# A new order list for the same operations in a fused retention and SwiGLU kernel

## The chip, the cores and the metric

The kernel runs on one core of a Trainium2 chip. A core has five engines with a queue each: TensorE (PE; its weight loads are listed apart as PEld), VectorE (DVE), ScalarE (ACT), GpSimd (POOL) and SyncE (SP), which here only issues transfers. The metric is the device time of one execution in microseconds (us); lower is better. The engines run their own lists in order and wait for each other through semaphores.

## The reference

```python
# q, k, v: (4 batches, 8 heads, 768 steps, 64), float32
state = gamma[None, :, None, None] * state + np.einsum('bhd,bhe->bhde', k[:, :, t], v[:, :, t])
y[:, :, t] = scale * np.einsum('bhd,bhde->bhe', q[:, :, t], state)
...
# x: y as (3072 tokens, 512)
rms = np.sqrt(np.mean(x * x, axis=-1, keepdims=True) + 1e-06)
xn = x / rms * rms_g
g = xn @ w_gate                       # 512 -> 1536
silu = g * (1.0 / (1.0 + np.exp(-g)))
return (silu * (xn @ w_val) @ w_out)  # 1536 -> 512
```

A recurrence with a decay gamma for each head, then a root-mean-square norm and a gated feed-forward layer.

## The kernel before, in words

The 768 steps are cut into six chunks c of 128 steps. Within a chunk the recurrence is computed in parallel form: scores of q against k under a decaying causal mask, times v, plus q times the state that earlier chunks left. A chunk has four batches b of 128 rows, so a tile is 128 rows by 512 columns (eight heads of 64). The feed-forward layer takes a chunk's four batches together: 512 rows. Its hidden width of 1536 is cut into 12 blocks n of 128.

There is no loop over this work. A string, ORDER (lines 17 to 99), is a list of 865 words, each one operation; a loop at the end (L604) takes word by word and emits its instructions. A word such as `v.0.0.2.2.3/4` has the operation, its indices and after a slash the PSUM banks; `@D`, `@A`, `@P` and `@S` name the engine (DVE, ACT, POOL, SP). The list thus sets, for every engine, the order of its queue. The words, with the lines that emit them:

- `Lq`, `Lk`, `Lv` c.b (L301 to L314): load q, k or v. On SP as float32 (tiles qf, kf, vf), on POOL with a cast to bf16 on the way (qb, kb, vp). For chunk 0, q and k that come through POOL are loaded in an eight-row form (L312) that needs a sort on PE.
- `Ck`, `Cq`, `V` (L335, L344, L350): casts of what SP loaded, with the decay for q and v from chunk 2 on.
- `Tk`, `Tq` (L362): transposes or sorts on PE, `Ek`, `Eq` (L375) copy the result out of PSUM as kT, qT. `tk`, `tq` (L386) are transposes by DMA, issued on SP. `J` (L507) turns a sorted kT back.
- `A` (L397) scores on PE, `M0` and `M1` (L422) the masked scores on DVE, `Y` (L433) and `Z` (L409) the outputs y on PE.
- `S`, `R`, `N` (L450, L462, L474): sum of squares on ACT, reciprocal root on POOL, normed row xn on DVE. `X` (L492) transposes xn on PE and `XE` (L499) copies it out; from chunk 2 on `XE@S` is a DMA transpose instead.
- `D` (L514) decayed k on DVE or POOL, `K` (L522) the new state's part on PE, `U` (L533) its sum and `B` (L541) its bf16 copy.
- `wg`, `wv`, `wo` (L323, L331): loads of the weights on POOL, in pieces. Every load of chunk 2 waits for the last piece of `wo` (L318).
- `g`, `v` c.n0.n1.b0.b1 (L548): feed-forward matmuls with the gate and value weights; `s` (L560) the silu on ACT, `h` (L566) the product on DVE. A stretch of blocks and batches can be cut small, so that it can start when one batch and one piece of weights are there.
- `d` (L574) the down projection on PE, `o` (L582) its copy out of PSUM, `st` (L589) the store by SP. `e` (L597) is the down projection of the last output block, cut into three column pieces.
- `H.n` (L236): n filler matmuls of 512 columns on PE that compute nothing that is used. `G` (L293) and `GE` spread the norm's weight over the rows. `causal`, `iota`, `ident`, `vd`, `yd`, `yt`, `mk0`, `mk1`, `mc`, `tab` make masks, decays and load the activation table.

Of the kernel before, what the change touches and what calls it, by code (L numbers as in the profile page):

```python
# [27 lines left out]
v.0.0.4.3.4/1 s.0.0.4.3.4 h.0.3.4.0.3 g.0.4.6.3.4/0 v.0.2.3.0.3/4 h.0.0.4.3.4 h.0.2.3.0.3 wg.9.12 g.0.5.6.0.3/5
s.0.4.6.3.4 D.0.2@P Lk.1.0@P B.0.0 g.0.4.5.0.3/7 s.0.5.6.0.3 wv.9.12 Tk.1.2/1 h.0.5.6.0.3 s.0.4.5.0.3
g.0.8.9.0.4/3 v.0.4.6.3.4/4 K.0.2.2/7 Tq.1.1/2 wo.0.4 g.0.6.7.0.4/0 Lv.1.1@P h.0.4.6.3.4 Ek.1.2@A g.0.7.8.0.4/1  # L30
Eq.1.1@D mc.1@D U.0.2.2@D h.0.4.5.0.3 D.1.1@P B.0.3 s.0.8.9.0.4 Tq.1.0/5 v.0.6.7.0.4/2 Tq.1.2/7 v.0.8.9.0.4/6
s.0.7.8.0.4 Eq.1.0@D Eq.1.2@D s.0.6.7.0.4 h.0.6.7.0.4 v.0.7.8.0.4/4 h.0.8.9.0.4 Lv.1.2@P A.1.2/70
g.0.10.11.0.4/6 Tk.1.0/1 Ek.1.0@A B.0.2 h.0.7.8.0.4 g.0.9.10.0.4/4 Lv.1.0@P M0.1.2 s.0.10.11.0.4 s.0.9.10.0.4
A.1.0/3572 M1.1.0 g.0.11.12.0.4/6 wo.4.8 M1.1.2 v.0.11.12.0.4/5 v.0.10.11.0.4/0 B.0.1 M1.1.1 wo.8.12
s.0.11.12.0.4 v.0.9.10.0.4/2 Lk.1.3@P Lq.1.3@P Lv.1.3@P d.0.1.0.4/4 h.0.11.12.0.4 Lq.2.0@S M0.1.1 Y.1.1/1
K.1.1/5 M0.1.0 S.1.1 h.0.10.11.0.4 Y.1.2/7 S.1.2 R.1.1 R.1.2 Lk.2.1@S D.1.0@P d.0.0.0.4/0 U.1.1@D Lk.2.3@S
h.0.9.10.0.4 Y.1.0/5 d.0.3.0.4/6 S.1.0 N.1.1 N.1.2 R.1.0 X.1.1/2 XE.1.1@D Lq.2.3@S d.0.2.0.4/3 D.1.2@P X.1.2/7
XE.1.2@A N.1.0 d.0.2.4.8 d.0.0.4.8 d.0.1.4.8 X.1.0/5 B.1.1 XE.1.0@D d.0.1.8.12 Lk.2.0@S o.0.1@A d.0.0.8.12
Tk.1.3/4 Ek.1.3@D g.1.0.1.0.3/1 v.1.0.1.0.3/2 Lq.2.1@S Tq.1.3/7 Eq.1.3@D o.0.0@A d.0.2.8.12 Lv.2.1@S K.1.0/4
s.1.0.1.0.3 h.1.0.1.0.3 A.1.3/51 M0.1.3 Ck.2.1@A tk.2.1 d.0.3.4.8 M1.1.3 g.1.3.4.0.3/7 Cq.2.0@P Y.1.3/0  # L40
s.1.3.4.0.3 U.1.0@D S.1.3 d.0.3.8.12 R.1.3 v.1.2.3.0.3/4 g.1.2.3.0.3/2 N.1.3 Lq.2.2@S o.0.3@A s.1.2.3.0.3
g.1.1.2.0.3/7 Ck.2.0@P X.1.3/5 s.1.1.2.0.3 h.1.2.3.0.3 Cq.2.3@D v.1.3.4.0.3/2 v.1.1.2.0.3/4 Lk.2.2@S XE.1.3@A
g.1.9.10.0.4/0 h.1.1.2.0.3 o.0.2@D h.1.3.4.0.3 g.1.5.6.0.4/5 Cq.2.1@P v.1.9.10.0.4/7 g.1.7.8.0.4/4 tq.2.0
Lk.3.0@S D.1.3@D g.1.11.12.0.4/3 v.1.7.8.0.4/6 V.2.1@D B.1.0 tq.2.1 s.1.5.6.0.4 tk.2.0 s.1.9.10.0.4 Ck.2.2@P
v.1.5.6.0.4/1 Ck.2.3@A Lq.3.0@S h.1.5.6.0.4 s.1.7.8.0.4 s.1.11.12.0.4 Lq.3.1@S Cq.2.2@P v.1.11.12.0.4/2 tk.2.3
tq.2.3 h.1.7.8.0.4 Ck.3.0@P h.1.9.10.0.4 g.1.6.7.0.4/0 h.1.11.12.0.4 s.1.6.7.0.4 v.1.6.7.0.4/3 Lv.2.0@S K.2.1/1
h.1.6.7.0.4 K.1.2.2/7 tq.2.2 A.2.0/2564 U.1.2.2@D g.1.0.4.3.4/3 M1.2.0 M1.2.1 Cq.3.1@P M0.2.1 v.1.8.9.0.4/0
g.1.8.9.0.4/5 g.1.4.5.0.4/6 Lk.3.1@S s.1.0.4.3.4 B.1.2 B.1.3 s.1.8.9.0.4 M0.2.0 tk.2.2 Y.2.1/3 S.2.1 h.1.8.9.0.4
v.1.0.4.3.4/4 v.1.4.5.0.4/0 U.2.1@D s.1.4.5.0.4 Cq.3.0@P R.2.1 v.1.10.11.0.4/6 g.1.10.11.0.4/2 h.1.4.5.0.4
h.1.0.4.3.4 Ck.3.1@P V.2.0@A N.2.1 tk.3.0 Y.2.0/5 s.1.10.11.0.4 h.1.10.11.0.4 Lv.2.2@S tq.3.1 A.2.2/4301  # L50
Lv.2.3@S M0.2.2 tk.3.1 V.2.2@P S.2.0 Lq.3.2@S M1.2.2 M0.2.3 d.1.1.0.10/2 d.1.1.10.12 M1.2.3 Y.2.2/3 R.2.0 S.2.2
d.1.2.0.12/1 N.2.0 R.2.2 V.2.3@D Y.2.3/4 d.1.0.0.10/0 XE.2.1@S Cq.3.2@P d.1.0.10.12 o.1.2@A S.2.3 N.2.2 R.2.3
# [587 lines left out]
```

## Time and profile before

| | |
|---|---|
| median of 3 runs (lowest to highest) | 232.96 us (232.46 to 233.1) |
| the profiled execution | 233.88 us |
| its span, first to last instruction | 232.1 us |
| TensorE busy | 224.2 us |
| granted TensorE clock, mean | 1.000 |
| moved between HBM and chip | 28.31 MB read, 6.29 MB written |

The profile is one execution. A row of the time line has the start, the duration, the engine and line, the operation with what it writes and reads, and how many; in brackets the idle time before it and what ended that. Durations of matmuls overlap, since PE is a pipeline: their pace is read from start to start. The chain of waits is followed back from the last instruction and has start, duration, engine, tile and line.

### The profile page before, as it was taken

What the parts mean: (1) busy time and instruction counts of PE and PEld (TensorE: products, weight loads), DVE (VectorE), ACT (ScalarE), POOL (GpSimd) and SP (SyncE); (2) the same over time, 40 slices, a digit from 0 to 9 for tenths busy, and PEclk for the clock granted to TensorE, in tenths of its full rate; (3) what the DMA queues carried; (4) which work ended last, traced back from release to release, by engine and by line L of the source; (5) the groups of instructions that cost most, each with busy time, mean ns of one, the idle gap of its engine ahead of it and who ended that gap; (6) DMA issues with size and microseconds to landing.
All of it is one profiled execution on the core that took longest, in us unless ns stands there. A gap on an engine that the chain in (4) does not pass through costs nothing.

```text
span 232.1 us, 4715 instructions
## 1 busy us (share of the span) xinstructions
PE 224.2 (97%) x1819; PEld 118.1 (51%) x1843; DVE 128.0 (55%) x233; ACT 90.1 (39%) x211; POOL 95.7 (41%) x169
## 2 busy tenths in 40 slices
...
DMA  6999999999879796989969769993861410001232
GB/s 121 150 168 157 187 182 187 199 179 227 182 158 139 158 219 105 240 172 227 197 138 222 205 129 198 248 133 70 123 197 23 120 64 0 0 0 48 109 133 76
DMA packets 105352, 33.60 MB, mean 145 GB/s; under 512 B 94449, under 2 KB 102385, under 8 KB 105330
## 3 DMA queue, kind: packets, MB, share of 16 engines
...
HBM read 28.31 MB, written 6.29 MB: 149 GB/s over the span
## 4 chain that ended last, share of the span: by engine, by line
PE 89%; POOL 3%; DVE 3%; DMA 3%; issue 1%; ACT 0%; POOLq 0%
PE g_ps L553 26%; PE o_ps L578 26%; PE v_ps L553 26%; DMA kb<-in_k_dram 3%; PE y_ps L442 2%; PE a_ps L405 2%; PE y_ps L446 2%; PE kv_ps L529 1%; PE o_ps L600 1%; POOL qb L312 1%; PE xt_ps L496 1%; DVE qT L382 1%; POOL vp L314 1%; DVE hT L571 1%; PE t_ps L373 1%
## 5 line engine op out<-in xcount | busy, mean ns | idle before, releaser
L571 DVE TENSOR_TENSOR hT<-sg,v_ps 128x512 bf16<-128x512 bf16 (+2 forms) x76 | 48.5, 655 | 52.9 <-PE v_ps L553 28.3
L563 ACT ACTIVATE sg<-g_ps 128x512 bf16<-128x512 f32 (+2 forms) x76 | 42.1, 574 | 77.9 <-PE g_ps L553 67.3
L553 PE MATMUL g_ps<-xnT,wg_b 128*128 128x512 bf16 (+2 forms) x335 | 70.0, 343 | 0.7 <-DVE hT L571 0.2
L553 PE MATMUL v_ps<-xnT,wv_b 128*128 128x512 bf16 (+2 forms) x336 | 69.9, 344 | 0.4
L578 PE MATMUL o_ps<-wo_b,hT 128*128 128x512 bf16 x269 | 63.0, 379 | 0.4
L553 PEld LDWEIGHTS <-wv_b 128*128 128x128 bf16 x344 | 30.7, 98 | 29.4 <-issue 0.2
L553 PEld LDWEIGHTS <-wg_b 128*128 128x128 bf16 x344 | 30.6, 98 | 29.5 <-DVE st_f L538 0.2
L578 PEld LDWEIGHTS <-hT 128*128 128x128 bf16 x276 | 26.2, 98 | 29.6 <-PE o_ps L578 0.5
L483 DVE SCALAR_TENSOR_TENSOR xn<-y_ps,rstd,g_bc 128x512 bf16<-128x512 f32 x22 | 16.5, 748 | 18.0 <-POOL rstd L471 18.0
L469 POOL TENSOR_SCALAR ms<-ssq 128x1 f32<-128x1 f32 x24 | 4.5, 190 | 46.3 <-ACT xsq L459 45.6
L427 DVE TENSOR_TENSOR am<-a_ps,causal 128x512 bf16<-128x512 f32 x32 | 20.2, 682 | 5.3 <-PE a_ps L405 5.3
L145 ACT COPY o_sb<-o_ps 128x512 f32<-128x512 f32 (+2 forms) x16 | 8.6, 549 | 37.2 <-PE o_ps L578 32.8
L545 POOL CAST st_b<-st_f 64x256 bf16<-64x256 f32 x40 | 17.3, 431 | 8.8 <-DVE st_f L538 6.3
L341 POOL TENSOR_TENSOR qb<-qf,ydec 128x512 bf16<-128x512 f32 x14 | 14.9, 1063 | 12.9 <-DMA qf<-in_q_dram 12.7
L459 ACT ACTIVATE xsq<-y_ps 128x512 f32<-128x512 f32 x22 | 13.1, 596 | 13.1 <-PE y_ps L446 12.7
L471 POOL TENSOR_TENSOR rstd<-ms,mhalf 128x1 f32<-128x1 f32 x24 | 13.2, 551 | 2.0
L145 DVE COPY o_sb<-o_ps 128x512 f32<-128x512 f32 (+1 forms) x10 | 6.5, 653 | 11.0 <-PE o_ps L578 8.2
L427 DVE TENSOR_TENSOR am<-a_ps,mask 128x512 bf16<-128x512 f32 x16 | 10.3, 683 | 2.7 <-PE a_ps L405 2.7
L145 POOL CAST kb<-kf 128x512 bf16<-128x512 f32 x9 | 5.9, 660 | 10.1 <-DMA kf<-in_k_dram 10.0
L442 PEld LDWEIGHTS <-am 128*128 128x128 bf16 x176 | 7.7, 98 | 3.9 <-issue 0.3
L442 PE MATMUL y_ps<-vp,am 128*128 128x64 bf16 x176 | 8.9, 193 | 0.2
L360 POOL TENSOR_TENSOR vp<-vf,vdec 128x512 bf16<-128x512 f32 x7 | 7.7, 1105 | 2.9 <-DMA vf<-in_v_dram 2.8
...
## 6 DMA issues: line engine op xcount, KB each, us to landing
out_dram<-o_sb SPq DMA_DIRECT2D x23, 256.0 KB, 2.5
kf<-in_k_dram SPq DMA_DIRECT2D x17, 256.0 KB, 3.8
vf<-in_v_dram SPq DMA_DIRECT2D x17, 256.0 KB, 4.0
qf<-in_q_dram SPq DMA_DIRECT2D x16, 256.0 KB, 3.4
...
qb<-in_q_dram POOLq DMA_DIRECT2D x8, 128.0 KB, 6.1
kb<-in_k_dram POOLq DMA_DIRECT2D x7, 128.0 KB, 6.2
vp<-in_v_dram POOLq DMA_DIRECT2D x7, 128.0 KB, 6.3
```

The costliest lines, as they stand in the source:

```text
L145: (e.copy if e is ACT else e.tensor_copy)(out, in_)
L341: e.tensor_tensor(out=u["qb"], in0=u["qf"], in1=ydec[:, c, :, None].to_broadcast([128, H, D]), op=ALU.mult)
L427: DVE.tensor_tensor(out=u["am"][:, i], in0=u["a"][i], in1=m, op=ALU.mult)
L442: nc.tensor.matmul(y[:, h, :], u["am"][:, h % 2, h // 2, :], u["vp"][:, h, :], start=h == 0, stop=c == 0 and h == H - 1, skip_group_check= ...
L459: ACT.activation(xsq, flat(u["y"]), AF.Square, accum_out=u["ssq"])
L471: POOL.tensor_tensor(out=u["rstd"], in0=ms, in1=mhalf, op=ALU.pow)
L483: DVE.scalar_tensor_tensor(out=u["xn"], in0=flat(u["y"]), scalar=u["rstd"], in1=g_bc, op0=ALU.mult, op1=ALU.mult)
L545: POOL.tensor_copy(st_b[b][r, :, i * 64:i * 64 + 64], st_f[b // 2][r, b % 2])
L553: nc.tensor.matmul(p[:, (n - n0) * m:(n - n0 + 1) * m], W[w][0][:, s, n * 128:(n + 1) * 128], xnT[c][:, s, b0 * C:b1 * C], start=s == 0, s ...
L563: ACT.activation(sg[:, :cols], done["wg", c, n0, b0][:, :cols], AF.Silu)
L571: DVE.tensor_tensor(out=hT[c][:, n0:n1, b0 * C:b1 * C], in0=sg, in1=p, op=ALU.mult)
L578: nc.tensor.matmul(o_ps[c, b], hT[c][:, n, b * C:(b + 1) * C], wo_b[:, n, :], start=n == 0, stop=n == NFF - 1)
```

## The change

Only ORDER changes: 867 words instead of 865. The operations on data are the same; order, banks and, for some fifty of them, the engine are others. The words that are not in both: fillers (`H`) are 17 matmuls before and 23 after.

The head of the list, cut to its start (the words up to the first feed-forward matmul and the first of those behind it):

```diff
-Lk.0.2@S causal Lv.0.2@S>causal rms.1@S Ck.0.2@D H.8/1 ident Lq.0.2@P vd Lk.0.1@P Lq.0.1@P Tk.0.2/2 Lq.0.0@P
-H.1/0 H.4/0 Tq.0.2/7 G/1 yd iota yt Lk.0.0@P mk0 Tk.0.1/6 Ek.0.2@D Lv.0.1@P mk1 Eq.0.2@D A.0.2/32 Lv.0.0@P
-Lk.0.3@P Tq.0.0/4 Tq.0.1/7 Lq.0.3@P GE@A M0.0.2 V.0.2@A wv.0.2 M1.0.2 wg.0.2 Ek.0.1@A Tk.0.0/1 Eq.0.1@A Eq.0.0@A
-Lk.1.1@P J.0.1/6 Y.0.2/5 Ek.0.0@D D.0.1@D S.0.2 R.0.2 A.0.0/0731 Lv.0.3@P M0.0.0 M1.0.0 H.2/2 Tk.0.3/2 tab
-M1.0.1 H.1/7 Y.0.0/7 Ek.0.3@A M0.0.1 H.1/2 Tq.0.3/2 N.0.2 J.0.0/3 S.0.0 Eq.0.3@A Y.0.1/0 wg.2.4 X.0.2/4 A.0.3/52
-R.0.0 N.0.0 J.0.3/1 XE.0.2@D S.0.1 X.0.0/6 wv.4.6 M1.0.3 v.0.0.2.2.3/4 R.0.1 g.0.0.2.2.3/7 XE.0.0@A Tk.1.1/6
...
+Lk.0.2@S H.4/4 yd causal Lv.0.2@S>causal yt rms.1@S ident Ck.0.2@A Lq.0.0@P H.8/1 Lq.0.1@P Lq.0.2@P Tk.0.2/7
+H.2/5 Lk.0.0@P Tq.0.1/0 vd Tq.0.0/4 Ek.0.2@D Lk.0.1@P Tq.0.2/1 Lk.0.3@P G/7 V.0.2@D Eq.0.1@D Tk.0.0/0 Tk.0.1/6
+Eq.0.2@D Eq.0.0@D iota Lq.0.3@P A.0.2/31 Lv.0.1@P mk0 Lv.0.0@P Lv.0.3@P Ek.0.0@D mk1 GE@A wg.0.2 M1.0.2 wv.0.2
+H.2/4 M0.0.2 Ek.0.1@A A.0.0/5270 D.0.2@P M1.0.1 Tk.0.3/6 Y.0.2/1 Tq.0.3/0 M0.0.1 H.2/4 tab Lk.1.1@P M1.0.0
+M0.0.0 S.0.2 Ek.0.3@A J.0.0/4 J.0.1/7 R.0.2 Y.0.1/2 Eq.0.3@A S.0.1 H.1/6 H.3/0 H.1/5 D.0.0@D Y.0.0/3 N.0.2
+J.0.3/5 D.0.1@D wv.2.4 R.0.1 X.0.2/6 N.0.1 S.0.0 wg.2.4 A.0.3/41 R.0.0 X.0.1/0 XE.0.2@A wg.4.6 D.0.3@D M0.0.3
+XE.0.1@A g.0.0.2.2.3/2 K.0.2.2/5 K.0.0.2/6 M1.0.3 U.0.2.2@A s.0.0.2.2.3 N.0.0 v.0.0.2.2.3/7 g.0.0.2.1.2/0
...
```

As the queues see it: POOL issues q of batches 0, 1 and 2, then k of 0, 1 and 3, q of 3, the three v, and then wg and wv (before: q 2, k 1, q 1, q 0, k 0, v 1, v 0, k 3, q 3, wv, wg, and v of 3 after k of the next chunk). The first twelve operations of PE are fillers. Later in the list:

- POOL's order of the remaining loads after k of chunk 1's batch 1: `wv.2.4 wg.2.4 wg.4.6 Lq.1.0 wv.4.6 wg.6.9 wv.6.9 Lk.1.2 Lk.1.0 wg.9.12 Lq.1.1 Lq.1.2 wv.9.12 wo.0.4 Lv.1.1 Lv.1.0 wo.4.8 wo.8.12 Lv.1.2 Lq.1.3 Lk.1.3 Lv.1.3`; before: `Lv.0.3 wg.2.4 wv.4.6 wv.2.4 wg.4.6 Lk.1.2 wg.6.9 Lq.1.1 wv.6.9 Lq.1.0 Lq.1.2 wg.9.12 Lk.1.0 wv.9.12 wo.0.4 Lv.1.1 Lv.1.2 Lv.1.0 wo.4.8 wo.8.12 Lk.1.3 Lq.1.3 Lv.1.3`.
- `mc.1` goes from DVE to POOL, `U.0.0.2` and `U.0.2.2` from DVE to ACT; `D.1.0` from POOL to DVE; `Ek.1.0` and `Ek.1.2` from ACT to DVE.
- On SP, chunk 4's four `XE@S` stand later among chunk 5's transposes: `XE.4.0 tq.5.1 tq.5.0 tk.5.1 XE.4.3 XE.4.2 XE.4.1 tk.5.0` (before: `XE.4.0 XE.4.1 XE.4.2 XE.4.3 tq.5.1 tk.5.0`, a v load, `tq.5.0 tk.5.1`). In the list two PE words (`v.4.8.9.0.4`, `Y.5.2`) stand between `tk.5.0` and `A.5.0`; before, `Y.5.2` and two feed-forward words stood between `tk.5.1` and `A.5.0`.
- The tail ends `d.5.2.0.12`, `e.5.3.0` (before: `d.5.2.0.12`, `e.5.3.2`, `e.5.3.0`).

More of the change, by code (lines that the diff above doesn't have):

```diff
@@ L28 @@
[L28 to L52, printed above, removed]
@@ new lines @@
+s.0.0.2.0.1 X.0.3/6 v.0.0.2.0.1/5 XE.0.3@A Lk.1.0@P B.0.0 wg.9.12 s.0.3.4.0.3 Lq.1.1@P g.0.5.6.0.3/1
+g.0.2.3.0.3/7 h.0.3.4.0.3 s.0.2.3.0.3 Lq.1.2@P h.0.2.3.0.3 g.0.4.5.0.3/0 wv.9.12 h.0.0.2.0.1 s.0.4.5.0.3
+v.0.0.4.3.4/2 g.0.0.4.3.4/7 v.0.4.5.0.3/3 mc.1@P s.0.5.6.0.3 s.0.0.4.3.4 h.0.0.4.3.4 wo.0.4 v.0.5.6.0.3/4
+h.0.5.6.0.3 D.1.1@P Lv.1.1@P h.0.4.5.0.3 Lv.1.0@P g.0.8.9.0.4/7 g.0.6.7.0.4/0 mc.0@D s.0.8.9.0.4 v.0.4.6.3.4/4
+g.0.4.6.3.4/5 s.0.4.6.3.4 v.0.8.9.0.4/6 D.1.0@D D.1.2@P wo.4.8 s.0.6.7.0.4 Tk.1.2/2 Ek.1.2@D Tq.1.0/5
@@ new lines @@
+N.1.1 d.0.1.0.4/0 R.1.0 d.0.2.0.4/5 N.1.0 X.1.1/3 d.0.2.4.8 d.0.0.4.8 Lv.1.3@P d.0.3.4.8 X.1.0/7 d.0.3.8.12
+XE.1.0@A Y.1.2/2 Tq.1.3/7 d.0.0.8.12 S.1.2 d.0.1.4.8 Lq.2.0@S XE.1.1@D o.0.0@A Eq.1.3@D o.0.3@A R.1.2 N.1.2
+Tk.1.3/1 d.0.2.8.12 X.1.2/3 Ek.1.3@A Ck.2.2@P D.1.3@D Lq.2.1@S A.1.3/17 XE.1.2@A M1.1.3 K.1.0/4 K.1.2.2/6
+K.1.1/2 B.0.3 M0.1.3 Lq.2.2@S tk.2.2 Ck.2.0@A g.1.0.1.0.3/3 v.1.2.3.0.3/7 U.1.1@D Y.1.3/1 s.1.0.1.0.3
+g.1.1.2.0.3/3 S.1.3 Lk.2.1@S g.1.3.4.0.3/2 o.0.2@A R.1.3 U.1.2.2@D d.0.1.8.12 Cq.2.1@P s.1.3.4.0.3 U.1.0@D
@@ new lines @@
+g.1.10.11.0.4/5 Cq.3.1@D Lv.2.2@S v.1.11.12.0.4/7 Cq.2.3@P h.1.5.6.0.4 s.1.11.12.0.4 B.1.3 h.1.11.12.0.4
+v.1.10.11.0.4/0 s.1.10.11.0.4 s.1.4.5.0.4 h.1.10.11.0.4 v.1.4.5.0.4/4 Cq.3.0@P h.1.4.5.0.4 g.1.7.8.0.4/5
+Lk.3.0@S A.2.0/4726 tq.2.3 tq.2.2 M0.2.0 v.1.7.8.0.4/0 Lv.2.3@S tq.3.1 Lk.3.2@S M0.2.1 s.1.7.8.0.4 M1.2.1
+g.1.6.7.0.4/1 h.1.7.8.0.4 M1.2.0 V.2.1@P v.1.6.7.0.4/5 Y.2.1/4 Ck.3.0@A s.1.6.7.0.4 S.2.1 K.2.1/0 tk.3.1 K.2.0/6
+V.2.2@P h.1.6.7.0.4 A.2.2/7231 M0.2.3 d.1.1.0.10/5 Lk.3.3@S V.2.3@P M1.2.3 tq.3.0 M1.2.2 d.1.1.10.12 R.2.1
@@ new lines @@
+M1.3.3 v.2.9.10.0.4/6 tk.4.1 g.2.10.11.0.4/7 Y.3.1/0 Cq.4.2@P h.2.0.1.0.4 s.2.9.10.0.4 S.3.1 Y.3.2/2
+s.2.10.11.0.4 st.1.0@S h.2.9.10.0.4 S.3.2 V.4.0@P h.2.4.5.0.4 Lq.4.3@S v.2.10.11.0.4/3 Lq.4.1@S Y.3.3/5 R.3.1
+h.2.10.11.0.4 v.2.11.12.0.4/1 N.3.1 S.3.3 g.2.11.12.0.4/4 s.2.11.12.0.4 R.3.2 Lv.5.1@S d.2.1.0.10/6 K.3.2.2/3
+R.3.3 N.3.2 XE.3.0@S K.3.0.2/0 Lk.4.0@S XE.3.2@S N.3.3 XE.3.1@S Lv.4.3@S XE.3.3@S h.2.11.12.0.4 Ck.4.0@A
+d.2.3.0.12/1 d.2.2.0.12/2 U.3.0.2@D g.3.0.1.0.4/4 v.3.0.1.0.4/7 Lq.4.0@S U.3.2.2@D st.0.2@S g.3.3.4.0.4/0
@@ new lines @@
+Ck.4.2@P s.3.3.4.0.4 st.0.1@S Lk.4.3@S Lv.5.0@S g.3.5.6.0.4/3 st.1.1@S B.3.1 v.3.3.4.0.4/0 d.2.1.10.12 tk.4.2
+g.3.4.5.0.4/5 Cq.4.3@P Cq.4.1@D s.3.0.1.0.4 Lq.5.3@S o.2.3@A h.3.0.1.0.4 h.3.3.4.0.4 s.3.5.6.0.4 o.2.1@D
+g.3.1.2.0.4/3 v.3.1.2.0.4/1 s.3.1.2.0.4 Ck.5.0@D o.2.2@D B.3.2 tq.4.2 V.4.3@P g.3.6.7.0.4/4 Lq.5.2@S V.4.2@P
+Cq.4.0@P v.3.6.7.0.4/3 s.3.6.7.0.4 tq.4.0 h.3.1.2.0.4 v.3.5.6.0.4/0 g.3.2.3.0.4/2 h.3.5.6.0.4 Lk.5.1@S
+h.3.6.7.0.4 tk.4.0 s.3.4.5.0.4 V.5.2@P tq.4.1 s.3.2.3.0.4 v.3.2.3.0.4/4 g.3.9.10.0.4/1 Ck.4.3@D v.3.4.5.0.4/0
@@ new lines @@
+g.4.5.6.0.4/2 v.4.9.10.0.4/4 v.4.1.2.0.4/7 XE.5.0@S st.3.3@S v.4.4.5.0.4/6 h.4.9.10.0.4 g.4.4.5.0.4/0
+s.4.1.2.0.4 g.5.3.4.0.4/3 st.3.0@S g.5.11.12.0.4/5 s.4.5.6.0.4 v.4.5.6.0.4/1 h.4.1.2.0.4 s.5.3.4.0.4
+g.5.9.10.0.4/3 g.5.0.1.0.4/2 s.4.4.5.0.4 h.4.5.6.0.4 g.5.7.8.0.4/1 s.5.7.8.0.4 v.5.7.8.0.4/0 h.5.7.8.0.4
+v.5.3.4.0.4/1 g.4.6.7.0.4/4 v.5.11.12.0.4/7 h.4.4.5.0.4 st.2.2@S h.5.3.4.0.4 s.5.11.12.0.4 s.4.6.7.0.4
+v.5.0.1.0.4/1 g.5.6.7.0.4/4 s.5.0.1.0.4 h.5.0.1.0.4 h.5.11.12.0.4 g.5.2.3.0.4/0 v.4.6.7.0.4/7 v.5.9.10.0.4/2
```

94 lines of the change are left out of this document (44 added, 50 removed).

## The prediction

> **What bounds the kernel now.** First the page's busy table, its DMA slices and its chain by engine: they name the bound and show where there is room.
>
> ```profile
> span 232.1 us, 4715 instructions
> PE 224.2 (97%) x1819; PEld 118.1 (51%) x1843; DVE 128.0 (55%) x233; ACT 90.1 (39%) x211; POOL 95.7 (41%) x169
> DMA  6999999999879796989969769993861410001232
> PE 89%; POOL 3%; DVE 3%; DMA 3%; issue 1%; ACT 0%; POOLq 0%
> ```
>
> PE is busy 97% of the span and carries 89% of the chain. The DMA row stands at 9 from slice 2 to slice 11, 6 to 64 us (a slice is 5.8 us): while weights and first inputs arrive, PE and the transfers are both full. Second, PE in order of time at the start.
>
> ```profile
> 1.11 3.59 PE L239 MATMUL hot_ps<-one 128*128 128x512 bf16 x8 [1.11 <-DVE one L152]
> 7.35 0.44 PE L368 MATMUL t_ps<-pick,qb 128*64 128x64 bf16 x16
> 7.72 1.12 PE L295 MATMUL g_row_ps<-g_row,ones 1*128 1x512 f32 x2
> 8.77 0.44 PE L368 MATMUL t_ps<-pick,kb 128*64 128x64 bf16 x16
> 9.15 0.40 PE L405 MATMUL a_ps<-qT,kT 64*128 64x128 bf16 x8
> 13.48 0.44 PE L368 MATMUL t_ps<-pick,kb 128*64 128x64 bf16 x16 [0.73 <-DMA kb<-in_k_dram]
> 17.52 0.61 PE L553 MATMUL v_ps<-xnT,wv_b 128*128 128x128 bf16 x8
> ```
>
> Until 17.52 PE runs fillers (L239) and the short attention work of chunk 0; from there a nearly unbroken line of matmuls to the tail. The order list gives both kernels the same work on PE except for fillers, 17 before and 23 after, all ahead of the first feed-forward matmul; and at that matmul both have done the same attention work (eight sorts of q and k, three J, all four A, three Y, two X). What PE has left there is equal. So the end moves by three amounts: the start of that matmul, what PE loses behind it, and the tail.
>
> Third, the chain of waits and PE's own rows where most is lost behind 17.52.
>
> ```profile
> 31.50 0.69 DVE qT L382
> 32.19 1.29 DVE mask L281
> ...
> 33.50 0.68 DVE st_f L145
> ...
> 37.09 1.02 PE g_ps L553 x4
> ...
> 39.19 0.55 PE a_ps L405 x16
> ...
> 224.13 2.59 PE o_ps L578 x12
> ```
>
> ```profile
> 31.30 1.89 PE L553 MATMUL g_ps<-xnT,wg_b 128*128 128x512 bf16 x8
> ```
>
> From 31.50 to 37.09 the chain runs through DVE, not PE. In the list PE has from 31.30 to 37.09 twenty feed-forward matmuls of 512 columns, two groups of four transposes and the eight matmuls of A.1.2. Back to back a 512-column matmul takes 2.59/12 = 0.216 us, a group of four a quarter of that per matmul (0.22), and eight of A half of 0.55. That makes 4.32 + 0.44 + 0.28 = 5.04 of 5.79 us: 0.75 us lost to DVE.
>
> **The change part by part.** *The front of PE.* Twelve fillers at 3.59/8 = 0.45 end at 1.11 + 5.4 = 6.5; the four transposes of batch 2's k and two more fillers (0.4 + 0.9) bring PE to 7.7. Before A.0.2 now stand three q sorts, the g row and two k sorts; before it was one, the g row and one. A sort takes 0.37 (7.35 to 7.72), 0.3 where PE is at speed; the g row 1.05 (7.72 to 8.77); A itself 0.3. A.0.2 thus ends between 10.5 and 10.9 instead of 9.5. The transfers do not set this, as issue times on POOL and the times from issue to landing show:
>
> ```profile
> 2.12 0.76 POOL L312 DMA_DIRECT2D qb<-in_q_dram  x1
> 2.88 0.54 POOL L312 DMA_DIRECT2D kb<-in_k_dram  x1
> ...
> 7.42 0.56 POOL L312 DMA_DIRECT2D kb<-in_k_dram  x1
> ...
> 9.24 0.79 POOL L325 DMA_DIRECT2D wg_b<-in_moe_w_gate_dram  x1
> ...
> 18.81 0.75 POOL L325 DMA_DIRECT2D wg_b<-in_moe_w_gate_dram  x1
> ```
>
> ```profile
> qb<-in_q_dram POOLq DMA_DIRECT2D x1, 128.0 KB, 4.3
> kb<-in_k_dram POOLq DMA_DIRECT2D x1, 128.0 KB, 4.2
> kb<-in_k_dram POOLq DMA_DIRECT2D x1, 128.0 KB, 6.0
> wg_b<-in_moe_w_gate_dram POOLq DMA_DIRECT2D x1, 256.0 KB, 7.7
> wg_b<-in_moe_w_gate_dram POOLq DMA_DIRECT2D x1, 256.0 KB, 6.0
> ```
>
> These belong to the five issues in the same order, so they land at 6.4, 7.1, 13.4, 16.9 and 24.8. The second place is now batch 1's q, which lands at about 7.1, before PE asks. Batch 3's k moves from eighth place to sixth: issued near 5.5, it lands at about 10.5 (a latency of 5, between 4.2 and 6.0). The 0.73 us that PE stood for it at 13.48 goes. What is late next is DVE.
>
> *DVE becomes the chain.* Its list, once A.0.2 is done, holds six mask products M, then D.0.0, N.0.2, D.0.1 and N.0.1; X.0.1 on PE waits for the last, and the first g stands behind X.0.1.
>
> ```profile
> 12.06 2.47 DVE L427 TENSOR_TENSOR am<-a_ps,mask 128x512 bf16<-128x512 f32 x4
> ```
>
> ```profile
> L483 DVE SCALAR_TENSOR_TENSOR xn<-y_ps,rstd,g_bc 128x512 bf16<-128x512 f32 x22 | 16.5, 748 | 18.0 <-POOL rstd L471 18.0
> L518 DVE TENSOR_TENSOR kd<-t_ps,vdec 128x512 bf16<-128x512 bf16 x3 | 2.0, 683 | 0.0
> ```
>
> Six M at 2.47/4 = 0.62 make 3.7, two D 1.37, two N 1.5, the four transposes X 0.22: 6.8 us. From 10.5 to 10.9 that gives a first g between 17.3 and 17.7; neighbours on DVE overlap by some 0.06 (four M in 2.47, not 2.73), which takes up to 0.5 off. I take 17.3, so 0.2 us earlier than 17.52, with bounds of 0.6 earlier and 0.4 later. The first wg has landed by then: batch 3's k at 13.42 ended 1024 KB of POOL's transfers and the wg at 16.94 ended 1664, 182 KB per us; it now ends at 1536 KB, 16.2.
>
> *Behind the start.* The two mask builds for chunk 1 (L281) are no longer both on DVE, the second is on POOL; the two copies of the state (L145, st_f) go to ACT, busy 39%. In the 31 to 37 us chain these are the rows of 1.29 and 0.68, 1.97 us in front of what PE waited for. What DVE takes in (D.1.0 and two copies of kT) stands earlier in its list or is the shorter. So the 0.75 us loss should go: I take all of it, with bounds of 0.75 and, if another DVE wait takes its place, nothing.
>
> Against this, weights have less lead. From 1664 KB at 16.94 to 24.8 came 1280 KB, 163 KB per us. By that rate the first wv, which now has batch 3's v and the wg ahead of it, ends at 17.6, 1.4 later than by the old order (it stood ahead of the wg), then, behind one k, wv, wg and wg of the next blocks at 20.0, 21.5 and 23.1. Counting PE's matmuls from a g at 17.3, they are asked for at 18.5, 21.0, 22.3 and 23.6. The lead is 0.5 to 1.0 us; where the list asks for later blocks (29 to 36 us) the same count leaves 0.1 to 0.5. A lead that thin will not always hold: I charge 0.3 us, with bounds of nothing and 1.75 (below).
>
> SP's loads of chunk 2 are gated by the last wo:
>
> ```profile
> 48.10 0.39 SPq L314 DMA_DIRECT2D qf<-in_q_dram  x1
> ```
>
> Now one 128 KB input fewer stands ahead of that wo (0.7 us at the rate above), and A.2.0 stands later in PE's list, so nothing waits longer there. The queue of SP behind it holds the same loads in another order.
>
> *The tail.* The last output block is written in pieces in both.
>
> ```profile
> 226.72 1.67 PE o_ps L600 x24
> 228.42 0.32 ACT o_sb L145
> ```
>
> ```profile
> out_dram<-o_sb SPq DMA_DIRECT2D x1, 96.0 KB, 2.3
> ```
>
> Now a whole 256 KB block's store starts some 0.7 us later against PE's end than before, just ahead of the 96 KB that ends the span (landing 2.3). Bounds: nothing, and 0.6 us later. I take nothing, since the two overlap.
>
> One rule speaks against the change.
>
> ```profile
> L312 POOL DMA_DIRECT2D qb<-in_q_dram x4: 547/660/995, 2.1 to 8.0; - x4
> ```
>
> ```profile
> L145 DVE CAST kb<-kf x1: 350/350/350, 4.2 to 4.2; 128x512 bf16<-128x512 f32 x1
> ```
>
> The same POOL issue of q takes 547 to 995 ns, and the long ones lie beside DVE's memsets and this cast. The Trainium skill, "SBUF — State Buffer", section "SBUF: two separate sides", says that a DMA issued from POOL waits for its descriptors while DVE copies fp32 within SBUF in a two-port mode. By that rule the v cast of batch 2, which moves to DVE, costs POOL's issues its 0.35 us, and the k cast that leaves DVE gives as much back: the sum would not move, and a weight lead of 0.1 to 0.5 would be touched. No row here shows a transfer late for it.
>
> **The sum.** Start 0.2 earlier, DVE's wait 0.75 less, thin leads 0.3 more, tail 0: 0.65 us off. The profiled execution took 233.88 us for its span of 232.1; it becomes 231.45 and 233.2. On the median of the three runs, 232.96, the same 0.65 us gives 232.3, which is the forecast.
>
> **The rivals.** *Weights come late, slower.* Transfers are the second full resource, and wv, wg, wg now queue behind ten inputs, not nine. If each takes the 7.7 us of a loaded queue and not 5 to 6, the weights that POOL issues near 14.1, 15.8 and 17.4 (counted from its rows of 0.5 to 0.9 us for an issue, with a pair of small operations for a reciprocal root ahead of each) land at 21.8, 23.5 and 25.1, and PE, asking at 21.0, 22.3 and 23.6, stands up to 1.5 us; with a start that is no earlier and a DVE wait that stays it comes to 232.96 + 1.5 - 0.2 = 234.3, with the DVE wait gone 233.5. It decides from a latency of 6.2 us (23.6 less 17.4) on. For it speaks the DMA row of nines; against it that later blocks came in 6.0 at the same full row. *A quicker front.* If PE reaches speed early and DVE starts M near 9.8, the start is bound by the wg at 16.2: 1.3 off, 231.3 with the other terms. Against it speaks the g row between the sorts. *It doesn't do what it says.* Batch 3's early k and q change nothing where ten DVE operations stand ahead of the first g: the start stays at 17.5 to 17.9 and DVE waits elsewhere: 233.0. *A late stall.* At chunk 5 the last k transpose on SP now comes directly behind the transposes of chunk 4's xn, which wait for DVE; before, four other words of SP came between.
>
> ```profile
> 152.09 7.97 SPq L502 DMA_TRANSPOSE xnT<-xn  x4
> ```
>
> Four of these took 7.97 us for their waits; if the last comes 1.5 us late, PE stands for A.5.0: 233.8. For it speaks the new place, against it that the other leads behind chunk 1 are as long as before or longer.
>
> **How the numbers follow.** Forecast 0.40 (its own range 231.7 to 232.9); weights late 0.25; quicker front 0.14; no effect 0.13; late stall 0.08. The measurement can tell about 0.3% from no change, so faster is below 232.26 and slower above 233.66. Faster: 0.28 of the forecast and 0.14 of the front, 0.42. Slower: 0.21 of late weights, 0.06 of the stall and 0.02 of no effect, 0.29. Within: 0.29. The range from 231.3 to 234.3 reaches from the front's time to the late weights'.
>
> **What would show it.** The first g_ps row at 17.3, behind an X that waits for xn on DVE; no PE wait on kb near 13; no DVE run of mask and st_f in the chain between 31 and 37 us; A.0.2 near 10.7. PE waits on wg or wv between 18 and 36 us would show the leads too thin. A first g after 18, a chain through DMA beyond 20 us, or a PE wait on kT near chunk 5 would make the forecast wrong.

## The result and the profile after

| | before | changed |
|---|---|---|
| median of 17 runs each (lowest to highest) | 232.96 us (232.41 to 233.53) | 232.12 us (231.88 to 233.8) |
| ratio, with its 95% interval | | 0.9975 (0.9964 to 0.9986) |
| the profiled execution | 233.88 us | 232.63 us |
| its span | 232.1 us | 230.7 us |

The changed kernel is faster by 0.25%, and the forecast of 232.3 us lies 0.2 us from its median. The sum came out; of its four terms one holds nearly as forecast, one cost twice its price, one failed and one is not shown, and a fifth was left out.

The page of the changed kernel: its span, the busy times and the chain by engine.

```profile
span 230.7 us, 4733 instructions
PE 223.7 (97%) x1822; PEld 119.3 (52%) x1849; DVE 128.7 (56%) x239; ACT 87.8 (38%) x197; POOL 92.8 (40%) x163
PE 93%; DMA 3%; issue 1%; DVE 1%; ACT 0%; POOL 0%; DVEq 0%
```

PE's share of the chain rises from 89% to 93%, DVE's falls from 3% to 1%. The time line of PE shows the new front.

```profile
1.11 5.30 PE L239 MATMUL hot_ps<-one 128*128 128x512 bf16 x12 [1.11 <-DVE one L152]
...
10.21 0.40 PE L405 MATMUL a_ps<-qT,kT 64*128 64x128 bf16 x8
...
11.63 0.44 PE L368 MATMUL t_ps<-pick,kb 128*64 128x64 bf16 x16
...
17.04 0.40 PE L496 MATMUL xt_ps<-ident,xn 128*128 128x128 bf16 x4 [0.40 <-DVE xn L483]
17.27 0.61 PE L553 MATMUL g_ps<-xnT,wg_b 128*128 128x128 bf16 x8
...
20.94 1.46 PE L553 MATMUL v_ps<-xnT,wv_b 128*128 128x384 bf16 x8
22.83 0.82 PE L553 MATMUL g_ps<-xnT,wg_b 128*128 128x384 bf16 x4 [0.43 <-DMA wg_b<-in_moe_w_gate_dram]
```

A.0.2 stands at 10.21, the wait on batch 3's k is gone (11.63), the first g stands at 17.27 behind an X that waited for xn, and one wait on weights has come, 0.43 us at 22.83. On DVE the six mask products begin at 10.73:

```profile
10.73 3.68 DVE L427 TENSOR_TENSOR am<-a_ps,mask 128x512 bf16<-128x512 f32 x6
```

The chain of the changed kernel in the stretch in which it used to run through DVE:

```profile
16.16 6.63 DMA wg_b<-in_moe_w_gate_dram
...
22.83 0.82 PE g_ps L553 x4
...
36.60 0.83 PE t_ps L373 x12
37.43 1.73 PE g_ps L553 x8
39.16 0.78 PE a_ps L405 x24
```

From 22.83 on it is PE alone, up to ACT's last copy. ACT's last copy, behind PE's last matmuls:

```profile
227.58 0.32 ACT L145 COPY o_sb<-o_ps 128x192 f32<-128x192 f32 x1 [0.36 <-PE o_ps L600]
```

From here to the end are 230.7 - 227.58 = 3.1 us; before, from the same copy at 228.42, they were 3.7. So of the 1.4 us between the two spans 0.55 lies behind the last copy, and 0.25 ahead of the first feed-forward matmul (17.52 to 17.27). The remaining 0.6 lies between: from the first feed-forward matmul to the last copy are 228.42 - 17.52 = 210.90 us before and 227.58 - 17.27 = 210.31 now.

### The profile page after: what moved, and what is told of

The parts are those of the page before. It is cut to its first block, busy times and chain, and to the rows that moved or that the text cites. A ratio compares the mean times of both kernels' runs of the same rounds, so it can differ in the third digit from the quotient of the medians.

```text
span 230.7 us, 4733 instructions
## 1 busy us (share of the span) xinstructions
PE 223.7 (97%) x1822; PEld 119.3 (52%) x1849; DVE 128.7 (56%) x239; ACT 87.8 (38%) x197; POOL 92.8 (40%) x163
## 4 chain that ended last, share of the span: by engine, by line
PE 93%; DMA 3%; issue 1%; DVE 1%; ACT 0%; POOL 0%; DVEq 0%
PE v_ps L553 26%; PE g_ps L553 26%; PE o_ps L578 26%; DMA wg_b<-in_moe_w_gate_dram 3%; PE hot_ps L239 3%; PE a_ps L405 3%; PE y_ps L442 2%; PE y_ps L446 2%; PE o_ps L600 1%; PE kv_ps L529 1%; PE t_ps L368 1%; PE t_ps L373 1%; DVE am L427 1%; PE xt_ps L496 1%; PE g_row_ps L295 0%
## 5 line engine op out<-in xcount | busy, mean ns | idle before, releaser
L571 DVE TENSOR_TENSOR hT<-sg,v_ps 128x512 bf16<-128x512 bf16 (+2 forms) x76 | 48.0, 655 | 54.4 <-PE v_ps L553 39.8
L578 PE MATMUL o_ps<-wo_b,hT 128*128 128x512 bf16 x265 | 62.3, 379 | 0.6 <-issue 0.2
L545 POOL CAST st_b<-st_f 64x256 bf16<-64x256 f32 x40 | 18.7, 467 | 6.7 <-DVE st_f L538 5.4
L341 POOL TENSOR_TENSOR qb<-qf,ydec 128x512 bf16<-128x512 f32 x13 | 13.7, 1055 | 10.5 <-DMA qf<-in_q_dram 10.2
L145 ACT COPY o_sb<-o_ps 128x512 f32<-128x512 f32 (+1 forms) x15 | 8.4, 567 | 23.5 <-PE o_ps L578 23.1
L145 DVE COPY o_sb<-o_ps 128x512 f32<-128x512 f32 (+2 forms) x11 | 6.7, 620 | 13.0 <-PE o_ps L578 7.3
L360 POOL TENSOR_TENSOR vp<-vf,vdec 128x512 bf16<-128x512 f32 x9 | 9.3, 1040 | 5.4 <-DMA vf<-in_v_dram 5.3
L239 PE MATMUL hot_ps<-one 128*128 128x512 bf16 x23 | 8.4, 516 | 1.1 <-DVE one L152 1.1
```

What stands on the lines that cost most here:

```text
L145: (e.copy if e is ACT else e.tensor_copy)(out, in_)
L239: nc.tensor.matmul(p, one, one[:, None, :].to_broadcast([128, 4, 128]), start=True, stop=True)
L341: e.tensor_tensor(out=u["qb"], in0=u["qf"], in1=ydec[:, c, :, None].to_broadcast([128, H, D]), op=ALU.mult)
L545: POOL.tensor_copy(st_b[b][r, :, i * 64:i * 64 + 64], st_f[b // 2][r, b % 2])
L571: DVE.tensor_tensor(out=hT[c][:, n0:n1, b0 * C:b1 * C], in0=sg, in1=p, op=ALU.mult)
L578: nc.tensor.matmul(o_ps[c, b], hT[c][:, n, b * C:(b + 1) * C], wo_b[:, n, :], start=n == 0, stop=n == NFF - 1)
```

## The experiments

Each ratio is to the kernel before, with its 95% interval. That kernel was run beside each experiment; its medians there were 232.94 to 233.17 us.

**One part alone: DVE's relief.** On the kernel before:

```diff
-U.0.0.2@D ... mc.1@D U.0.2.2@D
+U.0.0.2@A ... mc.1@P U.0.2.2@A
```

> The kernel before with one part of the change alone: the second mask build (mc.1) on POOL and the two state copies (U.0.0.2, U.0.2.2) on ACT instead of DVE. If the 1.97 us of these two rows on DVE are what PE loses 0.75 us for between 31 and 37 us, the time falls by about 0.75 us (ratio 0.997) and the first feed-forward matmul stays at 17.5. If another DVE wait takes their place, the time stays within 0.2 us of before and the chain still runs through DVE there.

232.12 us, 0.9958 (0.9941 to 0.9975). The chain in its profile, and PE's two ends of the stretch:

```profile
30.80 1.73 PE g_ps L553 x8
...
35.56 0.33 PE a_ps L405 x8
35.89 0.97 PE g_ps L553 x4
```

```profile
16.86 0.61 PE L553 MATMUL v_ps<-xnT,wv_b 128*128 128x128 bf16 x8
...
35.83 1.04 PE L553 MATMUL g_ps<-xnT,wg_b 128*128 128x512 bf16 x4
```

qT, mask and st_f are out of the chain. From the first v to this g PE takes 35.83 - 16.86 = 18.97 us; before it was 37.09 - 17.52 = 19.57. The jam was worth 0.60 us. This part alone is as fast as the whole change, but the jam is not all that it gains (0.92 us by the medians): only 230.3 - 227.18 = 3.1 us lie behind ACT's last copy here too, not 3.7, for a reason that the experiments on the tail below show (this kernel has three DVE instructions fewer).

**The change without that part.** On the changed kernel, `mc.1` and both `U` back to DVE.

> The changed kernel with the same three operations put back on DVE. If they cost what the first theory says, the changed kernel loses 0.4 to 0.75 us (0.4 where the wait for weights already covers a part) and stands within 0.3 us of before. If its gain comes from the start, the tail or elsewhere, it stays 0.5 to 0.9 us faster than before.

232.95 us, 1.0005 (0.9983 to 1.0027). The gain is gone, but it is lost at another place: PE's time line has its waits for DVE now at 20 to 22 us, where `U` stands ahead of batch 0's xn and xnT, and no jam at 31 to 37.

```profile
20.33 0.40 PE L496 MATMUL xt_ps<-ident,xn 128*128 128x128 bf16 x4 [0.27 <-DVE xn L483]
...
21.59 0.61 PE L553 MATMUL g_ps<-xnT,wg_b 128*128 128x128 bf16 x8 [0.19 <-DVE xnT L145]
```

So in this list the same load on DVE makes PE wait earlier. From start to start, the first g (17.51) to the g at 23.33 takes 5.82 us, and 4.97 in the kernel with the early weights below: the waits cost 0.85 there and hide the wait on weights, which alone costs 0.59 in the changed kernel (5.56). The profiles do not show all of the loss, though: from the first g to ACT's last copy this kernel is only 0.28 us longer than the changed one (210.59 against 210.31) and starts 0.24 later, while the medians differ by 0.8.

**Early k and q of batch 3 undone.** On the changed kernel:

```diff
-Lk.0.3@P ... Lq.0.3@P ... Lv.0.1@P mk0 Lv.0.0@P
+... Lv.0.1@P mk0 Lv.0.0@P Lk.0.3@P Lq.0.3@P
```

> The changed kernel with batch 3's k and q issued behind two of the v loads, as before. If their early place matters, batch 3's k lands at about 13.0 instead of 10.5, PE stands for it ahead of Y.0.2 for about 1.3 us, the norm chain of batch 2 starts later, and the first feed-forward matmul comes 0.6 to 1.3 us after 17.3; total up by as much. If DVE alone sets the start, the first matmul stays within 0.2 us of 17.3 and the total within 0.2 us of the changed kernel.

232.69 us, 0.998 (0.9962 to 0.9999), not told apart from the change as a whole. PE then waits 0.16 us for this k, and the first g is not later for it (16.97). But the k came at 11.5, not near 13.0 as expected, so the run does not tell what its early place is worth when it lands late.

```profile
11.55 0.44 PE L368 MATMUL t_ps<-pick,kb 128*64 128x64 bf16 x16 [0.16 <-DMA kb<-in_k_dram]
```

**Eight first fillers in place of twelve.** On the changed kernel, `H.4/4` taken out.

> The changed kernel with eight first fillers instead of twelve. If fillers only fill, PE reaches the first transposes at about 5.3 instead of 6.2 and the q sorts as each q lands (7.1, 7.3, 7.9 or so); A.0.2 starts 0 to 0.5 us earlier than 10.2 and the total falls by no more than that. If twelve are needed to bring PE to speed, the rows of the sorts and of A.0.2 grow to twice their length, A.0.2 starts later and the total rises by 0.3 us or more. The Trainium skill, TensorE: Matmul & The Clock Gate, Part 1, says that PE runs at half rate until one busy window of about 3.4 us has passed; by that rule a gap of 1 us at 5 us could keep PE slow for one more window.

234.83 us, 1.0063 (1.0038 to 1.0089). The windows from 0 to 17.5 us and from 8 to 10 us (length, PE, PEld, DVE, ACT and POOL busy, granted clock, DMA share, GB/s), then PE's time line:

```profile
0.00:17.50 17.50, 14.56 (x185) 7.62 (x185) 11.33 (x46) 11.45 (x26) 13.15 (x27) 0.80 1.19 143
```

```profile
8.00:10.00 2.00, 2.00 (x18) 0.89 (x18) 1.73 (x3) 0.36 (x2) 2.00 (x4) 0.50 1.42 174
```

```profile
5.57 0.59 PE L239 MATMUL hot_ps<-one 128*128 128x512 bf16 x2
7.26 1.27 PE L368 MATMUL t_ps<-pick,qb 128*64 128x64 bf16 x48 [1.09 <-DMA qb<-in_q_dram]
8.46 2.07 PE L295 MATMUL g_row_ps<-g_row,ones 1*128 1x512 f32 x2
...
19.53 0.61 PE L553 MATMUL g_ps<-xnT,wg_b 128*128 128x128 bf16 x8
```

PE had come to speed (two fillers in 0.59 us at 5.57), runs out of fillers, stands 1.09 us for q, and falls back to half speed: the granted clock is 0.50 from 8 to 14 us and 0.80 over the whole window, the g row takes 2.07 us (1.12 at speed), and the first g comes 2.3 us later. The Trainium skill, "TensorE: Matmul & The Clock Gate", section "Part 1: The HAM clock gate (the "warmup" mystery)", says that PE runs at half rate until a window of sustained work is full, and that this window runs freely, so that one kernel comes to speed after different counts of matmuls. The traces agree: the twelve first fillers take 5.30 us in the changed kernel and 4.24 in the kernel with `D.0.1` behind `N.0.1`, below, where the list up to them is the same. That kernel stood 1.34 us for q at the same place and kept its speed, so a gap of this length does not cost the speed each time.

**The wait for the third weight piece.** On the changed kernel, two loads earlier in POOL's queue:

```diff
-J.0.1/7 R.0.2 ... D.0.1@D wv.2.4 R.0.1 X.0.2/6 N.0.1 S.0.0 wg.2.4 A.0.3/41
+J.0.1/7 wv.2.4 R.0.2 ... D.0.1@D wg.2.4 R.0.1 X.0.2/6 N.0.1 S.0.0 A.0.3/41
```

> The changed list, with two of POOL's words moved: the load wv.2.4 ahead of R.0.2 and the load wg.2.4 ahead of R.0.1, so that both use POOL's idle time (0.89 and 0.43 us in the profile of the changed kernel). Theory (the wait of 0.43 us at 22.83 comes only from the place of wg.2.4 behind two R on POOL): wg.2.4 issues some 0.8 us earlier and lands before PE asks, the 0.43 us go, no other wait on weights comes; about 231.7. Rival (the rate of the transfers is the wall): the piece lands no earlier or the next piece is late instead; 232.0 to 232.2. Second rival: R comes later behind the issues and N with it; the first g is later by up to 0.6 and the time 232.5.

231.81 us, 0.9951 (0.9936 to 0.9965), the lowest median of all, from six executions; it is not told apart from DVE's relief alone. The piece is issued at 14.05 in place of 16.16, and PE takes it without a wait:

```profile
20.80 1.46 PE L553 MATMUL v_ps<-xnT,wv_b 128*128 128x384 bf16 x8
22.10 0.81 PE L553 MATMUL g_ps<-xnT,wg_b 128*128 128x384 bf16 x4
```

From the v ahead of it to this g are 1.30 us; in the changed kernel they were 22.83 - 20.94 = 1.89. By this pace the wait costs 0.59 us, more than the idle 0.43 of its row. Transfers were not the wall for this piece: POOL had stood 0.89 and 0.43 us for the sums of squares with the issue queued behind them.

**The g row earlier.** On the changed kernel, `G` in place of the two fillers `H.2/5`; then the same with the two early loads.

> The changed list, with the g row G put in the place of the two fillers H.2/5 behind the first k transposes, and taken out between the k and q sorts. It tests that the stretch up to A.0.2 sets the first feed-forward matmul through DVE. Theory: A.0.2 comes some 0.9 us earlier, DVE's M start near 9.9, the first g stands between 16.4 (where wg lands in the changed kernel) and 16.7; of that 0.6 to 0.8 the wait for wg.2.4, which lands at 22.8 whatever PE does, takes back all it can: net 231.9 to 232.1. Rival (DVE's copies of q and k, not PE, set the start of M): first g at 17.2 to 17.4 and 232.1. Second rival: fewer fillers keep PE slow for longer; first g after 17.8 and 232.7.

> Both edits together: the g row in place of two fillers, and wv.2.4 and wg.2.4 issued ahead of R.0.2 and R.0.1. Theory (the start is set by PE through DVE, and then by the weights' landing): first g at 16.5, no wait above 0.2 us at wg.2.4, 231.0 to 231.4. Rival (transfers are the wall from the first wg on): what is won at the start is waited for at 20 to 24 us, 231.8 to 232.1.

232.47 us, 0.9975 (0.9949 to 1.0002), and 231.94 us, 0.9969 (0.995 to 0.9989). The first g stands at 16.74 and at 17.10. The second is no gain on the early loads alone: A.0.2 came at 9.60, but DVE, with four casts of q and k in a row, began its mask products only at 10.56. So that rival holds in this kernel: DVE's casts, not PE, set the start of the mask products. In the first of the two they began at 10.20, after 0.16 us of waiting for A.0.2, so there it was still PE. The time line of DVE in the second:

```profile
8.16 1.89 DVE L145 CAST qT<-t_ps 128x512 bf16<-128x512 f32 x3 [0.67 <-PE t_ps L368]
9.97 0.68 DVE L145 CAST kT<-t_ps 128x512 bf16<-128x512 f32 x1
10.56 3.67 DVE L427 TENSOR_TENSOR am<-a_ps,mask 128x512 bf16<-128x512 f32 x6
```

Both kernels scatter more than the one with the fillers (231.7 to 234.69 and 231.55 to 233.74, against 231.62 to 232.72 in half as many executions). The two longest executions of the first and the five longest of the second have a granted clock of 0.985 to 0.993, the others 0.998 to 1.000.

**The tail's order alone.** On the kernel before:

```diff
-e.5.3.1/6 d.5.2.0.12/7 e.5.3.2/3 ... e.5.3.0/2
+e.5.3.2/3 ... e.5.3.1/6 ... d.5.2.0.12/7 e.5.3.0/2
```

> The kernel before, with the tail in the changed kernel's order alone: e.5.3.2 and its store ahead of e.5.3.1, so that only d.5.2 and e.5.3.0 end the list. Theory A (the 0.54 us by which the profiles differ behind PE's last matmul are the tail's order): the time falls by 0.4 to 0.6 us. Theory B (that difference is scatter of the last stores' landing): within 0.15 us of the kernel before. The one-part kernel with the tail of before showed 3.1 us from ACT's last copy to the end, as the changed kernel did, which speaks for B.

233.76 us, 1.0033 (1.0016 to 1.0051): slower, which neither theory had. Its rows, from PE's fillers, the first feed-forward matmul and ACT's last copy:

```profile
5.00 1.46 PE L239 MATMUL hot_ps<-one 128*128 128x512 bf16 x5
...
16.73 0.61 PE L553 MATMUL v_ps<-xnT,wv_b 128*128 128x128 bf16 x8
```

```profile
228.00 0.32 ACT L145 COPY o_sb<-o_ps 128x192 f32<-128x192 f32 x1 [4.26 <-PE o_ps L600]
```

Its span is 232.2 us: 4.2 us behind that copy. What stands in them is seen in the DMA view by queue (packets, MB, share of 16 engines). First that kernel, 229.5 to 230 us and then 230 to 230.5:

```profile
q1 hardware_dynamic: 48, 0.02, 16.8%
q14 instruction: 1, 0.01, 3.9%
...
q1 hardware_dynamic: 6, 0.00, 6.2%
```

Then the kernel before, 229 to 229.5 and 230 to 230.5 us:

```profile
q1 hardware_dynamic: 148, 0.07, 50.2%
q14 instruction: 1, 0.01, 3.9%
...
q1 hardware_dynamic: 12, 0.01, 6.0%
```

In both a packet of 8 KB of the instruction queue falls into the last stores, and after it the stores end in half a microsecond at 6% of 16 engines, which is what one engine alone would show while the others are done. In the changed kernel the packet comes at 211.8 us, with no store beside it:

```profile
q14 instruction: 1, 0.01, 24.9%
```

(0.1 us from 211.8.) In the twelve other profiles of this case the packet is not among the last stores, and there 3.1 to 3.2 us lie behind ACT's last copy with either order of the tail; only these two have 3.7 and 4.2. Where it falls goes with the number of DVE's instructions: 230 of them, 231.4 us (behind the last store); 233, 229.3 and 229.6; 239, 210 to 221; 242, 202.7.

**The instruction packet moved away.** Six memsets of an unused column on DVE, which it fits in near 206 us, in the kernel before and in the one with the tail's order:

```diff
-h.5.11.12.0.4 v.5.0.1.0.4/7
+h.5.11.12.0.4 PD.6 v.5.0.1.0.4/7
```

> The kernel before, with six memsets of one column of an unused tile on DVE, late in the list (behind h.5.11.12.0.4, near 205 us, where DVE is mostly idle). In the profiles of the kernel before and of the one with the tail's new order, an 8 KB packet of the instruction queue starts at 229.33 and 229.57, within the last stores, and one of 16 DMA engines is busy some 0.5 us longer than the rest; in the changed kernel that packet comes at 211.8 and the end is 3.1 us behind ACT's last copy, not 3.7. It moves with the number of DVE's instructions. Theory (the tail's half microsecond is this fetch): the packet comes 10 us or more earlier, the end comes 3.1 us behind ACT's last copy, 232.4 to 232.6. Rival (the packet costs nothing, the landing is scatter): 232.9 to 233.1.

> The kernel with the tail in the changed order (233.76 us against 233.0), with the same six memsets on DVE. Theory (the fetch falls within the last stores and the new order lets it hit the last 256 KB store): the packet comes earlier, the end comes 3.1 us behind ACT's last copy in place of 4.2, 232.4 to 232.8. Rival (the order of the tail itself costs 0.8 us, two stores late against each other): 233.6 to 233.8, and 4.2 us stay.

232.59 us, 0.9978 (0.9957 to 0.9998), and 232.57 us, 0.997 (0.9952 to 0.9987). Six operations more, and the kernel before is faster by half a microsecond, the other by 1.2 (by the medians; 1.5 by the ratios). The packet stands at 218.4 and 220.7; behind ACT's last copy (227.66 in a span of 230.8, 229.99 in one of 233.2) are 3.1 and 3.2 us. The first:

```profile
227.66 0.32 ACT L145 COPY o_sb<-o_ps 128x192 f32<-128x192 f32 x1 [0.68 <-PE o_ps L600]
```

So the order of the tail is worth nothing that these runs can tell, and the packet is worth about what the profiles differ by (0.5 and 1.0 us). The jam is still in the first of the two: from the first v at 16.74 to the g at 36.32 are 19.58 us.

**What sets the start.** On the kernel with the early loads, `D.0.1@D` behind `N.0.1`; then also `Y.0.1/2` ahead of the second `H.2/4`, `S.0.1` ahead of `Eq.0.3@A`, and `K.0.0.2/6` ahead of `K.0.2.2/5`.

> The changed kernel with the two weight loads issued early (231.81), and with D.0.1 on DVE behind N.0.1 in place of ahead of it. It tests that the row of DVE's operations ahead of X.0.1 sets the first feed-forward matmul. Theory: N.0.1 ends 0.68 us earlier and the first g stands at 16.5, bound now by wg's landing near 16.3; the state's part K, which needs D.0.1, waits nothing; wv at 17.7 and the next pieces wait 0 to 0.3; 231.2 to 231.5. Rival (transfers are the wall from the first wg on): what is won at the start is waited for at wv and at the next pieces, 231.7 to 231.9. Second rival: X.0.1 finds another wait (R.0.1 on POOL), first g at 17.0 and 231.8.

> The kernel with D.0.1 behind N.0.1, with three more words moved: Y.0.1 ahead of the two fillers H.2/4 and the two J on PE, S.0.1 ahead of Eq.0.3 on ACT, and K.0.0.2 ahead of K.0.2.2. In the kernel before this one X.0.1 still waited 0.41 us for xn on DVE, and DVE 0.57 for R.0.1 on POOL, which waited for the sum of squares on ACT and that for Y.0.1, which stands at 14.2 behind fillers though its masked scores are there at 13.3. Theory (two chains of equal length set the start, one through DVE, one through PE, ACT and POOL): with both cut, X.0.1 comes 0.4 us earlier, right behind A.0.3, the first g at 16.8 to 16.9; the wait of 0.35 for kd shrinks to 0.1; against the kernel before 0.9945 to 0.995, that is 231.9 if the kernel before is at 233.1. Rival (transfers are the wall from here on): the same start, but waits for wv and wg of 0.4 us at 17 to 23 us, ratio 0.9965 as it was.

232.42 us, 0.9965 (0.9949 to 0.9981), and 233.01 us, 0.9995 (0.998 to 1.001): both misses. In the first, DVE had only changed what it waits for:

```profile
16.23 0.75 DVE L483 SCALAR_TENSOR_TENSOR xn<-y_ps,rstd,g_bc 128x512 bf16<-128x512 f32 x1 [0.57 <-POOL rstd L471]
```

and the state's part on PE now waits 0.35 us for the late D. By these waits two chains of about the same length end in the first g, one through DVE and one through PE, ACT and POOL; the second run was to cut both and did not, so this stays a reading of the rows. In it, Y.0.1 was put ahead of work that had been hiding its wait:

```profile
13.66 0.39 PE L442 MATMUL y_ps<-vp,am 128*128 128x64 bf16 x8 [0.75 <-DVE am L427]
...
17.88 0.61 PE L553 MATMUL g_ps<-xnT,wg_b 128*128 128x128 bf16 x8 [0.21 <-ACT xnT L145]
```

PE stands 0.75 us with fillers and J queued behind the waiting Y, and the first g comes 0.61 us later than in the kernel before it (17.88 against 17.27). The expectation had read the masked scores as ready at 13.3; the row says 13.66, and it left out that PE takes its list in order.

## Why the prediction was right, and where it was not

**The start, -0.2 us: the path came, the gain is not shown.** The profiles give -0.25, by the steps foreseen (mask products at 10.73, foreseen 10.5 to 10.9; no wait on batch 3's k; X.0.1 behind xn). But the same old front starts its feed-forward work at 17.52 in the profile of before, at 16.86, 16.73 and 16.74 in three others, and at 18.98 in the kernel with the tail's order and the six memsets. The five fillers behind the k transposes do not explain it: they take 2.38 us in the first,

```profile
5.04 2.38 PE L239 MATMUL hot_ps<-one 128*128 128x512 bf16 x5
```

2.08 in the kernel that starts at 16.74, and 1.46 both where it starts at 16.73 and where it starts at 18.98. What moves it is the landing of batch 3's k. In the chains of before, of DVE's relief alone, and of the kernel that starts at 18.98:

```profile
7.42 6.02 DMA kb<-in_k_dram
13.48 0.44 PE t_ps L368 x16
...
7.43 5.35 DMA kb<-in_k_dram
12.83 0.44 PE t_ps L368 x16
...
7.43 6.81 DMA kb<-in_k_dram
14.29 0.64 PE t_ps L368 x16
```

In the first two 4.04 and 4.03 us follow to the first feed-forward matmul, and 4.04 in the kernel with the tail's order (12.69 to 16.73). In the third PE stood 2.49 us for the k and was slow behind it (0.64 us for a sort, 0.44 at speed). In the one that starts at 16.74 the k was there without a wait. The new front no longer hangs on this k. It starts at 17.27, 17.51, 17.13 and 17.27 where nothing ahead of the first g was moved on PE (16.97 with batch 3's k and q late): ahead of an old front whose k lands late, behind one whose k lands early. The profile of before is of the first kind, and at 233.88 us it is 0.9 above its kernel's median. What the twelve fillers do buy is a speed that holds, and the prediction did not price them: without four of them the kernel loses 2.7 us by the medians (2.1 by the ratios), and in nine of its twelve executions the granted clock is 0.978 to 0.993.

**DVE's jam, -0.75 us: right mechanism, somewhat less.** It is gone, and measured 0.60 in two pairs of profiles (19.57 and 19.58 against 18.97). The missing 0.15 us are in the reading of before: the 5.04 us of work in 5.79 were made from back-to-back durations, and PE loses a little at each change of operation even where it waits for nothing: with the jam gone the same stretch took 35.83 - 30.64 = 5.19.

**Thin leads, +0.3 us: right mechanism, one place, twice the price.** The leads that were worked out held except at wg.2.4, foreseen at 21.5, landed at 22.8: 0.59 us by the pace of PE. The step had its landing from the transfer rate; it was late because POOL stood for two sums of squares with the issue queued behind them. The rival that charged every piece with 7.7 us was nearer here than its price: the three pieces issued at 14.11, 16.16 and 17.84 landed after 5.8, 6.6 and 6.3 us. But the early loads took the whole wait away, so the rate of the transfers did not bind at this piece.

**What the sum left out, about -0.6 us.** The prediction calls what PE has left at the first feed-forward matmul equal. The work is equal, its time is not. From that matmul to ACT's last copy DVE's relief alone, which has no jam, takes 227.18 - 16.86 = 210.32 us; the changed list with the early loads, which has no wait on weights, takes 226.83 - 17.13 = 209.70. Most of the 0.62 lies where PE goes from its 128*128 matmuls to those of the scores (64*128) and of the state's part (128*64) and back. The state's part of two batches, first in the kernel before, which has a second such row at 30.69, then in the changed one:

```profile
22.27 0.44 PE L529 MATMUL kv_ps<-vp,kd 128*64 128x64 bf16 x16
...
17.81 0.69 PE L529 MATMUL kv_ps<-vp,kd 128*64 128x64 bf16 x32
```

From start to start, over what the matmul ahead takes, groups of 8, 16 and 24 score matmuls add 0.43, 0.65 and 0.87 us: eight more add 0.22, so each group costs 0.2 us beside its matmuls. Behind the first feed-forward matmul the old list has 16 stretches of such matmuls, the new one 13, and the same 336 matmuls take 10.93 us in DVE's relief alone and 10.46 with the early loads. This is read from profiles; no run tests it by itself.

**The tail, 0: this step failed.** It measured -0.55 us, outside its bounds of 0 to 0.6. The prediction looked at the order of the stores and at landings of 2.3 us; the order is worth nothing that the runs can tell. It did not see that in the profile of before a packet of code falls into the last stores, nor that adding six instructions to DVE (233 to 239) would take it out.

Behind the start the profiles show -0.60 (jam), +0.59 (wait on weights), -0.62 (left out) and -0.55 (tail): -1.18 us, where 0.84 was gained by the medians and 0.58 by the ratio. The first three make -0.63, and the stretch that they are in measured 210.31 - 210.90 = -0.59. What is missing to the medians fits a new front that starts 0.3 to 0.6 us later than the usual old one; that is an estimate from the starts above. So the forecast of -0.65 was close by luck: a gain at the start that is not shown and a wait priced at half stood against a tail of -0.55 and a gain of about 0.6 that were not in the sum. Six idle memsets alone give about what the new list gives (0.9978 against 0.9975). The rivals fell: a quicker front did not come, the change does what it says, and chunk 5 has no stall (behind 23 us no wait of PE in the changed kernel is for data). Two readings in the prediction are off, and neither moves the forecast: the DMA row stands at 9 to slice 10 (58 us), not 11, and the sum of late weights takes 0.2 us off for a start that it calls no earlier, while its bound of 1.75 has no working.

Open stay two things. That the packet is DVE's code is inferred from its moving with DVE's count; the trace does not name the engine. And how often batch 3's k lands late in the old front, and so which front starts earlier in the middle of many executions, would need more profiles than were taken.
